# Mixers, channel weights and q tails fetched by GpSimd transfers that cast to fp16, in a fused attention and phase-mixing kernel

## Chip, cores and metric

One core of one Trainium2 chip. The metric is the device time of one execution in microseconds (us); lower is better.

## What is computed

Inputs are fp32. q, k and v have the shape batch 8, heads 8, sequence 576, head width 64. The matrices are theta and channel (512 x 512) and the two token mixers r and i (576 x 576). The reference, cut to what matters:

```python
kv = np.einsum('bhsd,bhse->bhde', k, v)          # linear attention
out = np.einsum('bhsd,bhde->bhse', q, kv)
rms = np.sqrt(np.mean(out * out, axis=-1, keepdims=True) + 1e-06)
x = out / rms * g_norm                           # then heads side by side: (8, 576, 512)

theta = x @ w_theta
zr, zi = x * np.cos(theta), x * np.sin(theta)
y = np.einsum('ts,bsd->btd', w_tok_r, zr) + np.einsum('ts,bsd->btd', w_tok_i, zi)
u = x + y
result = u + np.maximum(u @ w_ch, 0.0)
```

## The kernel before, in words

**Tiles.** A batch's 576 rows are four tiles of 128 and a tail of 64. Heads go in four pairs. For each pair kv is a product of fp32 k and v (L549). q is cast to fp16 into `qcast` (cast_q, L498, its tail L504, from the staging tile `ql`) and turned (`qT`): for batches 0 to 3 on TensorE (L645, tail L778), from batch 4 on by transposing DMAs (L519, L525). Then, by tile, come the product raw (L582), its square on ScalarE (sq), the sum on VectorE (ss), the power -1/2 on GpSimd (rt, L600 and L604; batch 0 uses a square root on ScalarE and a reciprocal instead), the scaled x (L616) and its transpose `xT` (L805, L814). Batches 0 and 1 do this by pairs of heads for the four full tiles (by_pair, with names like raw0h, sq1h, rt1h, xTps1h), and by tile for the tail alone. `phase` makes theta (`th`, L858, L863), rounds it with `pt` on ScalarE (L870) and `f` and `fa` on VectorE, takes two sines on ScalarE (`tr`, L893, tail L901) and multiplies (`z`, L911). `mix` sums `y` over the mixers (L954) and adds x (`uT`, L965). `channel` multiplies uT by `wch` (`vps`, L1012), turns uT back (`ups`, L1003, copied to `u`, L1019; for batches U_FROM = 4 to 6 by transposing DMAs, L1041, into `ub`), adds (`ot`, L1023) and stores (L1030, L1035).

**Weights.** `chunk` (L404) loads each weight in fp32 pieces on SP's queue into eight staging slots `wst`: four of theta, five for each mixer, four of the channel matrix. `cast` writes each piece to fp16 on ScalarE (L414), VectorE (L416) or GpSimd (L420): theta to `wth`; a mixer's first 512 columns to `wnat` (rows 512 to 575: `wnatl`) and its last 64 columns to `wtt`; the channel matrix to `wch`. `mixer_step` turns the mixers on TensorE (`wTps`, L477) and copies them to the nine tiles `wT` (L487).

**Order.** Nothing is ordered by hand. `Weave` (L59) is a planner that runs while the program is built: each step has costs on one or several engines, a due time from the table DUE, what it needs, and the buffers that it takes and frees. It picks step by step, with a model of engines and DMA, and `in_traced_order` then ties every engine to this order. At run time an engine that waits holds all that stands behind it in its order. SP issues all loads, stores and DMA transposes, at most eight in flight in the plan's model; loads keep the order of their due times. [...]the square root serves batch 0's norms, and the sine table is loaded once (`table`, L461) after all five square roots of batch 0, its tail's included. Products with no use (`warm`, L340) fill the gaps of TensorE up to a planned time, to keep its clock up.

**Loads before.** SP issues batch 0 (q, k, v of four pairs), then theta's four pieces with q, k, v of batch 1's first pair between them, batch 1's q tail, the five pieces of mixer r, batch 0's q tail, mixer i, the rest of batch 1, the first pair of batch 2 and its tails, the channel matrix, and so on.

Of the kernel before, what the change touches and what calls it, by code (L numbers as in the profile page):

```python
# [17 lines left out]

PERIOD = 26.33
START = 4.0  # L20
DUE = {
    "load": (-15.39, 8.44),
    "theta": (0.94, 0),
    "mixers": (12.3, 6.02),
    "wch": (33.66, 6.0),
    "wT": (20.94, 1.64),
    ("phase", 0): (19.67, 0.63),
    ("mix", 0): (28.29, 4.94),
    ("channel", 0): (31.53, 7.53),
    ("phase", 1): (11.06, 3.64),  # L30
    ("mix", 1): (31.8, 5.47),
    ("channel", 1): (54.0, 10.9),
    ("first", 1): (-21.76, 0.88),
    "first": (-9.27, 0),
    "cast": (27.66, 1.46),
    "turn_q": (-15.49, 0.49),
    "attention": (-2.25, 1.53),
    "norm": (0.56, 4.11),
    "turn": (5.47, 0.91),
    "phase": (18.31, 3.54),  # L40
    "mix": (52.55, 3.41),
    "channel": (67.54, 4.08),
}
# [3 lines left out]
    "rt": 6, "x": 9, "xT": 3, "pt": 2, "f": 2, "fa": 2, "tr": 2, "uT": 2, "u": 3, "ub": 1, "ot": 3,  # L47
    "wst": 8, "z0": 2, "z1": 2, "z2": 2, "z3": 2, "z4": 2,
}
BANK = {"th": "mm", "y": "mm", "vp": "mm", "pu": "tp", "px": "tp"}  # L50
QUAD = 2
Q_DMA = 4
U_FROM = 4
X_FROM = 8
MIX_AFTER = 3
WCH_AFTER = 8


class Weave:  # L59
# [7 lines left out]

    SLACK = {"PE": 0.141, "ACT": 0.031, "DVE": 0.084, "POOL": 0.1, "SP": 0.05}
    MARGIN = {"PE": 0.027, "ACT": 0, "DVE": 0.564, "POOL": 0.1, "SP": 0.0}
    LANES = 8  # L70
    BEGIN = {"PE": 1.6, "ACT": 3.2, "DVE": 1.7, "POOL": 2.5, "SP": 0.73}
    WARM = 72.3
    COLD = 5.0
    URGENT = 5.7
    AHEAD = 0.27
    HOLD = 3.61
    DRAIN = 0.095
# [21 lines left out]
    def run(self):  # L99
        done, free, last = {}, dict(self.BEGIN), {}  # L100
        dma_free, port_free, log = 0.0, 0.0, []
        landed = [0.0] * self.LANES
        hot, streak, form = False, self.BEGIN["PE"], 0
# [21 lines left out]
        while ready:  # L125
            best = {}
            for t in ready:
                (name, engines, due, fn, needs, makes, uses, dma) = t
                if any(not self.slots[tag] for (tag, _) in makes):
                    continue  # L130
                at = max([done[n] for n in needs], default=0.0)
                for (tag, _) in makes:
                    at = max(at, min(self.slots[tag]))
                if dma is not None:
                    at = max(at, landed[-self.LANES])
                for (e, cost, lat, port) in engines:
                    new = e == "PE" and self.ARRAY[port] != form
                    clear = free[e] + self.DRAIN if new else free[e]
                    start = max(clear, at + self.MARGIN[e], port_free if port is True else 0.0)
                    if name[0] == "warm" and start > self.WARM:  # L140
                        continue
                    if due < self.URGENT:
                        start = max(clear, start - self.AHEAD)
                    best.setdefault(e, []).append(
                        (start, due + self.HOLD * new, max(at, port_free) if port is True else at, t, cost, lat, port)
                    )
# [32 lines left out]
            if dma is not None:  # L179
                (first, took) = dma  # L180
                dma_free = max(start + first, dma_free) + took
                end = dma_free + 0.2
                landed.append(end)
            done[name] = start + cost if name[0] == "warm" else end
# [34 lines left out]
def kernel(  # L219
# [75 lines left out]
    for i in range(2):  # L295
        kl = const.tile([P, H, D], FP32, tag=f"kl{i}", name=f"kl{i}")
        vl = const.tile([P, H, D], FP32, tag=f"vl{i}", name=f"vl{i}")
        for t in (kl, vl):
            nc.gpsimd.memset(t[T:P], 0.0)
        tails.append((kl, vl))  # L300
    gcol = const.tile([P, 1], FP32, tag="gcol")
    root_d = const.tile([1, 1], FP32, tag="root_d")
    nc.vector.memset(root_d[:], math.sqrt(D))
    wth = wpool.tile([P, NK, C], FP16, tag="wth", name="wth")
    wch = wpool.tile([P, NK, C], FP16, tag="wch", name="wch")
    wnat = [wpool.tile([P, NF, SF], FP16, tag=f"wnat{i}", name=f"wnat{i}") for i in range(2)]
    wnatl = [wpool.tile([P, SF], FP16, tag=f"wnatl{i}", name=f"wnatl{i}") for i in range(2)]
    wtt = wpool.tile([P, NT, 2, T], FP16, tag="wtt", name="wtt")
# [22 lines left out]
    def dma(took):  # L331
        return (1.85, took)

# [13 lines left out]
    def load(b, hp):  # L347
        pair = slice(2 * hp, 2 * hp + 2)

        def part(kind, src):  # L350
            def fn(e):
                if kind == "q" or b >= QUAD:
                    t = sb(kind, [P, 2, NF, D], FP32, f"{kind}{b}_{hp}")
# [25 lines left out]
        for (i, (kind, src)) in enumerate((("q", q), ("k", k), ("v", v))):  # L379
            full = kind == "q" or b >= QUAD  # L380
            weave.add((kind, b, hp), [sp(0.47)], due("load", b, hp) + 0.01 * i, part(kind, src),
                      makes=[(kind, f"{kind}{b}_{hp}")], dma=dma((0.82 if full else 0.78) + (1.0 if (kind, b, hp) == ("v", 0, 0) else 0)), load=True)
        if hp == (0 if b else HP - 1):
            for (i, (kind, src)) in enumerate((("kl", k), ("vl", v), ("ql", q))):
                if b < QUAD and kind != "ql":
                    continue
                weave.add((kind, b), [sp(0.64)], due("load", b, hp) + (0.04 if b else 1.15) + 0.01 * i,
# [6 lines left out]
    def load_weights():  # L394
# [31 lines left out]
        at = due("load", 0, HP - 1) + 1.0  # L426
        mixers = due("load", MIX_AFTER // HP, MIX_AFTER % HP) + 1.0
        for kc in range(NK):
            chunk(("wst", kc), moe_w_theta[kc * P:(kc + 1) * P, :], at + 0.01 * kc)
            cast(("wth", kc), ("wst", kc), wth[:, kc, :],  # L430
                 lambda kc=kc: st["wst", kc][:, 0:C], due("theta", 0, kc), FOLD)
        use = due("mixers", 0, 0)
        for (i, w) in enumerate((moe_w_tok_r, moe_w_tok_i)):
            for j in range(NT):
                name = ("wmix", i, j)
                rows = P if j < NF else T
                chunk(name, w[0:SF, :].rearrange("(p j) s -> p j s", j=NF)[:, j, :] if j < NF
                      else w[SF:S, :], mixers + 0.1 + 0.1 * i + 0.01 * j)
                cast(("wnat", i, j), name, wnat[i][:, j, :] if j < NF else wnatl[i][0:T],
                     lambda name=name, rows=rows: st[name][0:rows, 0:SF], use + i)  # L440
                cast(("wtt", i, j), name, wtt[0:rows, j, i, :],
                     lambda name=name, rows=rows: st[name][0:rows, SF:S], use + i)
        for kc in range(NK):
            chunk(("wcs", kc), moe_w_ch[kc * P:(kc + 1) * P, :],
                  due("load", WCH_AFTER // HP, WCH_AFTER % HP) + 1.4 + 0.01 * kc)
            cast(("wch", kc), ("wcs", kc), wch[:, kc, :],
                 lambda kc=kc: st["wcs", kc][:, 0:C], due("wch", 0, kc))

# [16 lines left out]
    def mixer_step(n):  # L465
# [16 lines left out]
        def keep(e):  # L482
# [3 lines left out]
            else:  # L486
# [3 lines left out]
        weave.add(("wTps", n), [pe(0.282)], at, turn,  # L490
                  needs=[("wnat", n // NF, j) for j in range(NT)] if n < 2 * NF
                  else [("wtt", i, j) for i in range(2) for j in range(NT)], makes=[("tp", name)])
        weave.add(("wT", n), [act(S), dve(0.38, True)], at, keep, needs=[("wTps", n)], uses=[name])


    def cast_q(b, hp):
# [6 lines left out]
        def tail(e):  # L503
            nc.vector.tensor_copy(qcast[b % 2][:T, NF], st["ql", b][:])  # L504

        first = [("qc", f"qc{b}")] if hp == 0 else []
        more = [] if hp == 0 else [f"qc{b}"]
# [3 lines left out]
                  uses=[f"q{b}_{hp}"] + more)  # L511
        if hp == 0:
            weave.add(("qcl", b), [dve(0.33, True)], at + (0.1 if b else 9.0), tail,
                      needs=[("ql", b)], uses=[f"ql{b}", f"qc{b}"])
# [123 lines left out]
    def turn_q_pair(b, hp, at):  # L638
# [3 lines left out]
        def turn_q0(e):  # L642
            t = st[pq] = ps("tp", [P, SF], FP16, pq)
            for j in range(NF):
                nc.tensor.matmul(  # L645
                    t[:, j * P:(j + 1) * P], qcast[b % 2][:, j, pair, :], ident16[:],
                    is_transpose=True, start=(j == 0), stop=(j == NF - 1),
                )

        def keep_q0(e):  # L650
# [6 lines left out]
            else:  # L657
                nc.vector.tensor_copy(t, src)

        weave.add((pq,), [pe(0.226)], at, turn_q0, needs=[("qc", b, hp)], makes=[("tp", pq)],  # L660
                  uses=[f"qc{b}"])
        weave.add(("qT", b, hp), [act(SF), dve(0.35, True)], at, keep_q0, needs=[(pq,)],
# [324 lines left out]
    def channel(b, ti):  # L987
# [64 lines left out]
        elif ti == 0:  # L1052
            for kc in range(NK):
# [5 lines left out]
        weave.add((vp,), [pe(0.866) if full else pe(0.436, "H")], at + 0.01, product,  # L1059
                  needs=uTs + [("wch", kc) for kc in range(NK)] + ([] if pu_on else us),  # L1060
                  makes=[(BANK["vp"], vp)], uses=[f"uT{b}"])
# [68 lines left out]
```

## Time and profile before

| | |
|---|---|
| median of 18 runs | 218.98 us (217.85 to 221.1) |
| the profiled execution | 218.53 us, span 216.7 us |
| granted TensorE clock | 1.000 |
| DMA | 46.82 MB, mean 216 GB/s; SP's queue busy for 76.9% of 16 engines' span |
| loads of q, k, v: 256 KB each | 4.8 to 5.5 us from issue to landing |
| `ql` loads: 8 of 128 KB in pieces of 256 bytes | 5.0 us |
| GpSimd instructions in all | 93, of which 35 are powers of 1.75 us |

The table's DMA times are medians from issue to landing, and contain the queue: eight transfers share the 16 DMA engines. In the time lines of the profile a row has the start and the length in us, the engine (SPq is SP's queue), the line, the operation, the tile written and the tile read, and the shape. In the lists of groups a row ends with busy time, mean length in ns, and idle time in front of it with what ended it. TensorE's products are pipelined, so the sum of groups is more than the engine's own time.

### The profile page before, as it was taken

Reading aid. Unit: us, or ns where it says so; the run is one execution under the profiler, and the core shown is the slowest. Engines: PE = TensorE matmul, PEld = TensorE weight load, DVE = VectorE, ACT = ScalarE, POOL = GpSimd, SP = SyncE. Lnnn points to the kernel's source line nnn. Section 1 sums busy time; section 2 is a strip of 40 time slices with the busy share of each in tenths; the row PEclk is TensorE's granted clock in tenths of the full one; section 3 lists DMA queues with packets and bytes.
Section 4 is the critical chain, followed back from the end, with each engine's and each line's share of the span. In section 5 each row is a group of like instructions: output and inputs, shape, how many; then the busy total and the mean of one; then the engine's idle time right before and its main releaser. Section 6 shows DMA issues by size and latency. Waiting matters only on the chain.

```text
span 216.7 us, 5976 instructions
## 1 busy us (share of the span) xinstructions
PE 204.1 (94%) x2361; PEld 144.0 (66%) x2361; DVE 181.9 (84%) x368; ACT 154.9 (71%) x304; POOL 80.4 (37%) x93
## 2 busy tenths in 40 slices
PE   7688789999999999999999999999999999999992
PEld 5575347875767666876776776866675756677560
DVE  2296789899989899989998999999899899973652
ACT  2185989987993979889859997886886776930031
POOL 8001510762025630773257425655454763000000
PEclk9999999999999999999999999999999999999999
DMA  5999799999977988999896989992723232525524
GB/s 202 367 382 294 242 332 346 197 352 327 242 249 218 260 281 266 158 292 301 242 222 175 330 254 204 266 292 64 156 53 145 77 73 60 185 48 51 194 75 167
DMA packets 59007, 46.82 MB, mean 216 GB/s; under 512 B 29156, under 2 KB 50660, under 8 KB 58980
## 3 DMA queue, kind: packets, MB, share of 16 engines
q1 hardware_dynamic: 58976, 46.45, 76.9%
q8 instruction: 18, 0.29, 0.6%
q14 instruction: 9, 0.07, 0.1%
q10 hardware_dynamic: 4, 0.00, 0.0%
HBM read 33.06 MB, written 9.44 MB: 196 GB/s over the span
## 4 chain that ended last, share of the span: by engine, by line
PE 63%; ACT 12%; DVE 8%; DMA 8%; POOL 4%; issue 2%; SPq 0%; DVEq 0%; ACTq 0%
PE y L954 25%; PE vps L1012 13%; PE th L858 8%; PE kv L549 6%; DMA wst<-in_moe_w_theta_dram 3%; DMA k<-in_k_dram 3%; PE xTps L805 3%; PE raw L582 3%; ACT pt L870 2%; PE ups L1003 2%; DMA v<-in_v_dram 2%; ACT tr L893 2%; DVE ss L593 2%; POOL rt1h L717 2%; ACT tr L901 2%; DVE x L616 2%
## 5 line engine op out<-in xcount | busy, mean ns | idle before, releaser
L954 PE MATMUL y<-wT,z 128*128 128x320 f16 (+1 forms) x576 | 77.3, 286 | 0.4 <-DVE uT L965 0.4
L954 PEld LDWEIGHTS <-z 128*128 128x128 f16 x576 | 54.9, 98 | 16.4 <-issue 1.2
L604 POOL TENSOR_TENSOR rt<-ss,mhalf 128x8 f32<-128x8 f32 x31 | 54.3, 1752 | 2.6
L1012 PE MATMUL vps<-wch,uT 128*128 128x512 f16 (+1 forms) x192 | 36.5, 344 | 0.0
L965 DVE SCALAR_TENSOR_TENSOR uT<-y,gcol,xT 128x320 f16<-128x320 f32 (+1 forms) x48 | 29.2, 611 | 7.0 <-PE y L954 6.9
L600 POOL TENSOR_SCALAR ss<-ss 128x8 f32<-128x8 f32 x31 | 9.6, 309 | 68.5 <-DVE ss L593 67.7
L858 PE MATMUL th<-wth,xT 128*128 128x512 f16 x128 | 31.7, 379 | 0.7 <-DVE f L874 0.7
L870 ACT ACTIVATE pt<-th,magic_t 128x512 f32<-128x512 f32 (+1 forms) x40 | 25.7, 642 | 6.7 <-PE th L858 5.7
L1019 ACT COPY u<-ups 128x512 f16<-128x512 f16 (+1 forms) x28 | 14.4, 520 | 19.5 <-PE ups L1003 19.3
L874 DVE SCALAR_TENSOR_TENSOR f<-pt,th 128x512 f32<-128x512 f32 (+1 forms) x40 | 24.9, 626 | 2.9 <-ACT pt L870 2.5
L549 PE MATMUL kv<-v,k 128*64 128x64 f32 (+1 forms) x672 | 25.3, 222 | 2.2 <-DMA v<-in_v_dram 2.2
L549 PEld LDWEIGHTS kv<-v,k 128*64 128x64 f32 (+1 forms) x672 | 22.4, 136 | 6.7 <-issue 4.6
L814 ACT ACTIVATE xT<-xTps,gcol 128x512 f16<-128x512 f16 (+1 forms) x32 | 20.1, 630 | 7.9 <-PE xTps L805 7.8
L893 ACT ACTIVATE tr<-fa,pio_t 128x512 f16<-128x512 f32 x32 | 22.7, 718 | 1.8 <-DVE fa L881 1.7
L616 DVE TENSOR_TENSOR x<-raw,rt 128x512 f16<-128x512 f32 x32 | 21.8, 682 | 2.5 <-POOL rt L604 2.3
L593 DVE TENSOR_REDUCE ss<-sq 128x8 f32<-128x512 f32 x32 | 21.5, 677 | 2.4 <-ACT sq L589 2.1
L893 ACT ACTIVATE tr<-f 128x512 f16<-128x512 f32 x32 | 19.7, 630 | 3.2 <-DVE f L874 3.1
L1012 PEld LDWEIGHTS <-uT 128*128 128x128 f16 (+1 forms) x192 | 14.8, 102 | 10.3 <-issue 0.2
L911 DVE TENSOR_TENSOR z<-x,tr 128x1024 f16<-128x1024 f16 (+1 forms) x32 | 19.5, 616 | 0.8 <-ACT tr L893 0.4
L1023 DVE SCALAR_TENSOR_TENSOR ot<-vps,u 128x512 f32<-128x512 f32 (+1 forms) x28 | 17.0, 606 | 2.4 <-PE vps L1012 2.0
L858 PEld LDWEIGHTS <-xT 128*128 128x128 f16 x128 | 11.4, 98 | 11.4 <-ACT xT L814 1.2
L589 ACT ACTIVATE sq<-raw 128x512 f32<-128x512 f32 x32 | 18.8, 592 | 0.0
(103 smaller groups left out, 259.4 us busy)
## 6 DMA issues: line engine op xcount, KB each, us to landing
q<-in_q_dram SPq DMA_DIRECT2D x32, 256.0 KB, 5.5
out_dram<-ot SPq DMA_DIRECT2D x32, 256.0 KB, 2.5
k<-in_k_dram SPq DMA_DIRECT2D x24, 256.0 KB, 5.2
v<-in_v_dram SPq DMA_DIRECT2D x24, 256.0 KB, 4.8
k<-in_k_dram SPq DMA_DIRECT2D x8, 288.0 KB, 6.0
v<-in_v_dram SPq DMA_DIRECT2D x8, 288.0 KB, 6.1
wmix<-in_moe_w_tok_r_dram SPq DMA_DIRECT2D x4, 288.0 KB, 6.8
wmix<-in_moe_w_tok_i_dram SPq DMA_DIRECT2D x4, 288.0 KB, 3.7
```

Source lines behind the costliest of these rows:

```text
L549: nc.tensor.matmul(kvp[r * D:(r + 1) * D, hp, :], kt, vt, start=(j == 0), stop=(j == (NT if b >= QUAD else NS) - 1),)
L593: nc.vector.reduce_sum(out=t[:], in_=st[sq][:].rearrange("p (h e) -> p h e", h=H), axis=mybir.AxisListType.X,)
L604: nc.gpsimd.tensor_tensor(out=r[:], in0=t[:], in1=mhalf[:], op=ALU.pow)
L616: nc.vector.tensor_tensor(out=t[:].rearrange("p (h e) -> p h e", h=H), in0=st[raw][:].rearrange("p (h e) -> p h e", h=H), in1=st[rt][:].un ...
L814: nc.scalar.activation(out=st["xT", b][:, :, cols], in_=st[px][:, :, 0:cols.stop - cols.start], func=AFT.Copy, scale=gcol[:],)
L858: nc.tensor.matmul(t[:], xT[:, kc, :], wth[:, kc, :], start=(kc == 0), stop=(kc == NK - 1),)
L870: nc.scalar.activation(out=t[:], in_=st[th][:], func=AFT.Identity, bias=magic_t[:])
L874: nc.vector.scalar_tensor_tensor(out=t[:], in0=st[pt][:], scalar=MAGIC, in1=st[th][:], op0=ALU.subtract, op1=ALU.subtract,)
L893: nc.scalar.activation(out=t[:, which, :], in_=src[:], func=AFT.Sin, scale=-RAD, bias=0.0 if bias is None else bias[:],)
L954: nc.tensor.matmul(st[y][:, c, :], z[:, kc * P:(kc + 1) * P], wT[m][:, cols], start=(c == 0 and m == 0) if open_sums else m == 0, stop=m = ...
L965: nc.vector.scalar_tensor_tensor(out=st["uT", b][:, chunks, cols], in0=st[y][:], scalar=gcol[:], in1=st["xT", b][:, chunks, cols], op0=ALU ...
L1012: nc.tensor.matmul(t[half], uT(kc), wch[:, kc, r * n:(r + 1) * n], start=(kc == 0), stop=(kc == NK - 1),)
```

## The change

The mixers, the channel matrix and the q tails of batches 2 to 7 come by DMAs that GpSimd issues and that cast on the way, straight into the fp16 tiles. The staging pieces of the mixers and of the channel matrix are gone, and so are their casts; `wst` has four slots for theta alone. `wnat` now holds all 576 columns; the last 64 are copied on chip to `wtt`, in two steps for each mixer. A mixer is two transfers (128 partitions x 2304 elements, and 64 x 576), the channel matrix two, a q tail one: twelve in all. A `hold`, a copy of one column from a named v tile, stands in GpSimd's order ahead of the mixers (v of batch 0, pair 2) and of the channel matrix (v of batch 2, pair 0), so that they are issued only when that tile has landed. The q loads themselves stay on SP (Q_SOFT = 0).

The planner's DMA model gets a second queue (`Transfers`): GpSimd's transfers run at half pace, and SP's at half pace beside them. The planner's due times and its other constants are changed too, and with them the whole order: theta's four pieces and batch 0's q tail now come directly behind batch 0, then the rest of batch 1 and batch 2. Batch 3's output is now turned by DMA as well (U_FROM 3).

In the built program GpSimd's order is: hold, mixer r (two transfers), mixer i (two), two wtt copies of mixer i, two powers of batch 1, hold, the q tail of batch 2, the two channel transfers, the other powers of batch 1, and from there powers with the q tails of batches 3 to 7 between them. ScalarE has all four theta casts, and ahead of its first and second `pt` the two wtt copies of mixer r.

```diff
-U_FROM = 4
+U_FROM = 3
-MIX_AFTER = 3
+MIX_AFTER = 2
 WCH_AFTER = 8
+Q_SOFT = 0
+QL_SOFT = 1
...
-    "wst": 8, "z0": 2, "z1": 2, "z2": 2, "z3": 2, "z4": 2,
+    "qh": 6, "wst": 4, "z0": 2, "z1": 2, "z2": 2, "z3": 2, "z4": 2,
...
+    def soft(took):
+        return (2.4, took, True)
+
+    def hold(name, due, after):
+        def fn(e):
+            t = st[after]
+            nc.gpsimd.tensor_copy(late[:], t[:, 0, 0:1] if len(t.shape) == 3 else t[:, 0, 0, 0:1])
+        weave.add(name, [("POOL", 0.2, 0.22, False)], due, fn, needs=[after],
+                  uses=["{}{}_{}".format(*after)])
...
+                if kind == "ql" and QL_SOFT and b > 1:
+                    def fetch(e):
+                        nc.gpsimd.dma_start(
+                            out=qcast[b % 2][0:T, NF], in_=q[b, :, SF:S, :].rearrange("h s d -> s h d")
+                        )
+                    weave.add(("qcl", b), [("POOL", 0.56, 0.56, False)], due("load", b, 0), fetch,
+                              needs=[("qc", b, 0)], uses=[f"qc{b}"], dma=soft(0.9))
                     continue
...
-            for j in range(NT):
-                name = ("wmix", i, j)
-                rows = P if j < NF else T
-                chunk(name, w[0:SF, :].rearrange("(p j) s -> p j s", j=NF)[:, j, :] if j < NF
-                      else w[SF:S, :], mixers + 0.1 + 0.1 * i + 0.01 * j)
-                cast(("wnat", i, j), name, wnat[i][:, j, :] if j < NF else wnatl[i][0:T],
-                     lambda name=name, rows=rows: st[name][0:rows, 0:SF], use + i)
-                cast(("wtt", i, j), name, wtt[0:rows, j, i, :],
-                     lambda name=name, rows=rows: st[name][0:rows, SF:S], use + i)
...
+            def main(e, i=i, w=w):
+                nc.gpsimd.dma_start(
+                    out=wnat[i][:], in_=w[0:SF, :].rearrange("(p j) s -> p j s", j=NF)
+                )
+
+            def rest(e, i=i, w=w):
+                nc.gpsimd.dma_start(out=wnatl[i][0:T], in_=w[SF:S, :])
...
+            weave.add(("wnat", i), [("POOL", 0.56, 0.56, False)], use + 0.1 + i, main,
+                      needs=["hold_mix"], dma=soft(3.4))
+            weave.add(("wnatl", i), [("POOL", 0.56, 0.56, False)], use + 0.2 + i, rest,
+                      needs=["hold_mix"], dma=soft(0.5))
+            weave.add(("wtt", i, 0), [act(P * 2), dve(0.3, True), pool(P * 2)], use + 8, part(0),
+                      needs=[("wnat", i)])
+            weave.add(("wtt", i, 1), [act(T), dve(0.1, True), pool(T)], use + 8, part(1),
+                      needs=[("wnatl", i)])
...
+        for h in range(2):
+            def fetch(e, h=h):
+                nc.gpsimd.dma_start(
+                    out=wch[:, 2 * h:2 * h + 2, :],
+                    in_=moe_w_ch[h * SH:(h + 1) * SH, :].rearrange("(k p) c -> p k c", p=P),
+                )
```

## The prediction

> **What bounds the kernel now.** I read the page's busy shares first, then the busy time of each engine in stretches of 10 us, then the time lines of SP, ScalarE, GpSimd and VectorE over the first 45 us, then the chain that ended last. Shares first:
>
> ```profile
> PE 204.1 (94%) x2361; PEld 144.0 (66%) x2361; DVE 181.9 (84%) x368; ACT 154.9 (71%) x304; POOL 80.4 (37%) x93
> L340 PE MATMUL warm<-kvbd 128*128 128x256 f16 x42 | 10.1, 315 | 3.0 <-DVE root_d L303 1.5 <-ACT kvbd L678 0.7 <-DVE f L874 0.3
> ```
>
> TensorE is busy for 94%, and 10.1 us of that is the filler product (warm), which computes nothing. Where the rest is lost is told by the stretches (columns: PE, weight load, DVE, ACT, POOL busy, clock, DMA share, GB/s):
>
> ```profile
> 0.00:10.00 10.00, 6.75 (x96) 5.27 (x97) 2.52 (x13) 1.54 (x3) 4.89 (x15) 1.00 0.79 276
> 10.00:20.00 10.00, 8.65 (x164) 6.62 (x162) 8.41 (x20) 7.37 (x21) 0.62 (x1) 1.00 1.07 348
> 20.00:30.00 10.00, 8.14 (x73) 4.55 (x71) 7.12 (x15) 8.77 (x21) 4.07 (x8) 1.00 0.90 268
> 30.00:40.00 10.00, 9.03 (x166) 6.83 (x165) 8.71 (x22) 9.26 (x21) 0.92 (x3) 1.00 1.15 307
> 50.00:60.00 10.00, 10.00 (x139) 6.79 (x138) 9.69 (x21) 8.85 (x17) 0.12 (x1) 1.00 0.98 278
> 190.00:200.00 10.00, 10.00 (x81) 7.73 (x79) 5.41 (x10) 1.48 (x3) 0.00 (x0) 1.00 0.40 54
> ...
> ```
>
> The reader is to see two regimes. Up to 40 us TensorE has gaps, ScalarE is the fullest engine and the DMA engines are full. From 50 us on TensorE is at 9.6 to 10.0 in every stretch, so a cast saved on VectorE or ScalarE there moves nothing. The end is set by when the full regime begins and by how much TensorE work it holds. In the start-up, SP and ScalarE show why it begins late:
>
> ```profile
> 12.27 0.33 SPq L404 DMA_DIRECT2D wst<-in_moe_w_theta_dram x1
> 13.81 4.14 SPq L404 DMA_DIRECT2D wmix<-in_moe_w_tok_r_dram x5
> 21.07 0.62 SPq L373 DMA_DIRECT2D ql<-in_q_dram x1
> ```
>
> ```profile
> 23.63 1.14 ACT L414 ACTIVATE wnat<-wmix 128x512 f16<-128x512 f32 x2
> 30.12 1.28 ACT L461 ACT_TABLE_LOAD   x1
> 32.35 1.14 ACT L893 ACTIVATE tr<-f 128x512 f16<-128x512 f32 x2
> ```
>
> The q tail of batch 0 is issued only at 21.07, behind five mixer chunks that waited for staging slots. Through it the tail's norm is late (its product raw at 27.99), through that the switch to the sine table (30.12), and every sine waits for the table: the first at 32.35, the last about 43.0.
>
> **The part that removes work.** ScalarE loses six wnat casts (0.63 us each) and three wtt (0.25): 4.5 us between 21.6 and 29.7, then three wch (1.8 us). It gains two theta casts (it now has all four, 0.63 each) and two wtt copies (0.3 and 0.2 estimated from their 256 and 64 columns beside wtt's 0.25). VectorE loses 1.4 us of mixer casts, one theta cast (0.37) and six of eight q-tail casts (6 x 0.41 = 2.5 us); GpSimd loses 3.6 us of casts. On the path I count only what falls before the sines; q-tail casts lie under full TensorE and count nothing (if that cover were gone: 2.5 us). SP loses 20 issues.
>
> **The part that moves loads.** The first twelve loads are the same and end at 13.01. Loads land 0.75 us apart (11.52, 12.26, 13.01). Theta's last chunk landed at 19.32, with three loads of batch 1 between the chunks. Now the four chunks follow batch 0 directly: 16.0 if alone, 19.0 if the mixers take half of the DMA engines from about 13. Batch 0's q tail is next: 20 to 21 instead of 24.26. The mixers start when v of pair 2 has landed (about 10.8, between its neighbours' 9.99 and 11.52) plus a tiny GpSimd copy and the time from issue to first data, for which I take 2 us: 13. DMA moved 350 to 380 GB/s there; at half of that, the first mixer's 1.18 MB takes 6.5 us and lands at 19.6 to 20.5, the second at 27 to 28, before: 29.6. All of q, k, v of batch 1 come ahead of where they were (the total is 10.6 MB at 350 GB/s, about 31 us, against 36.6).
>
> **The new start-up, step by step.** In the built program's order the first theta product waits for the last x transpose. That stood behind a kv product of batch 1 that waited for its load (18.59); this kv now comes after the theta products. I take th at 20.3 instead of 20.94. ScalarE's first pt is ready at 21.3; the wtt copy now ahead of it waits for the first mixer (20.5), just hidden. Three th at 0.86 us, the tail's transpose, the fourth th: tail product raw at 24.0 instead of 27.99. From raw to the table took 2.1 us, and there is one more qT copy (0.5) ahead now: table at 26.7, first sine at 28.4 instead of 32.35. That is 4 us gained, but not all is kept: from the first to the last sine ScalarE took 10.6 us nearly without idle time, and the built order puts two wT copies, one xT, one sq and one qT copy more into that stretch (five at 0.5 to 0.58, 2.7 us). Last sine at about 41.7 instead of 43.0; ScalarE is the bound of the start-up, and what is late next is batch 1's last pair (square on ScalarE, sum on VectorE, 2.0 us of power on GpSimd, scale, transpose), by the same count 46 instead of 49.03.
>
> As a marker I take the first theta product of batch 1, at 50.35. Counting every product issued before it at the pace the trace shows (0.86 us for four of 512 columns, 1.22 for nine of 320, 1.05 for 36 small kv), 29.5 us of TensorE work lay before it and 28.9 lie before it now. By the chain above it comes at 47.7: 2.65 earlier, less 0.6 of work not yet done, 2.05. The other marker, the last step of the first two y sums (45.6, with 25.0 done), comes at 42.3 with 25.2 done: 3.4. I take the middle, **-2.8 us**.
>
> **TensorE work.** Batch 3's output transposes move from TensorE to DMA (U_FROM 4 to 3): four groups of four products, 0.22 each in the chain of waits, **-0.9 us**, on the full engine. Against it stand four VectorE adds that read the transposed tile (684 instead of 606 ns, 0.3 us, hidden) and four transposes on SP (2.5 us to land each), ahead of the next loads; batches 4 to 6 already do this without TensorE gaps, so I take nothing.
>
> **Waits added.** Twelve transfers now stand in GpSimd's queue. Behind each q tail is a pair of power instructions (0.31 + 1.75 us) for which VectorE's x waits. All x waits for rt total 2.3 us in the whole run, and GpSimd is busy for 37%. The trace of before has no GpSimd transfer; the bound from above is 1 us for each of six issues, 6 us, from below 0. The nearest row is SP's own issue of a q tail, 0.62 us, and a TensorE that has other products ready, so I take 0. The hold before wch stands in front of the last two powers of batch 1 until v of batch 2 lands (41.41 before, about 36 now); the powers are due near 39 to 41, so it is hidden; if that load came no sooner, it would cost some 2 us.
>
> One rule speaks against this change. VectorE and GpSimd already stop each other in this trace:
>
> ```profile
> 26.39 0.79 DVE L504 CAST qcast<-ql 64x512 f16<-64x512 f32 x1
> ```
>
> ```profile
> 26.29 0.62 POOL L420 TENSOR_SCALAR wnat<-wmix 128x512 f16<-128x512 f32 x1 [0.31 <-DMA wmix<-in_moe_w_tok_i_dram]
> ```
>
> This cast takes 0.41 us elsewhere; here it waited for the GpSimd cast beside it, 0.38 us. The Trainium skill, "SBUF — State Buffer", the box on the "DVE blocks DMA" trap, says more: descriptors of GpSimd's transfers are written through the port that VectorE's two-port modes lock, and a transfer of some 620 ns alone became 3100 ns beside a copy. By the row a transfer starts at most 0.4 us late and the first mixer lands at 20.9: no loss. By the rule it starts 2.5 us late, at 15.5, lands at 23, and the pt queue behind the wtt copy slips 1.7 us: the sum would be 217.0. No run here shows the rule; I go by the row, since VectorE's instructions are short[...], and keep 217.0 in the range.
>
> **Sum.** The profiled execution took 218.53, of which 216.7 is the span. -2.8 - 0.9 = -3.7: span 213.0, execution 214.8. The median of the runs is 218.98, 0.45 above the profiled one: **215.3**.
>
> **Rivals.** (1) *The casting transfer is slow* (slower than before). If the DMA engines pass cast data at half the pace, the first mixer needs 13 us and lands at 26.5. ScalarE's wtt copy then holds all four pt, th is out of slots, the table and every sine follow: 5.2 us after 21.3, 220.5. It decides from a landing of 21.3 + 3.7 = 25.0. For it: nothing in the trace shows a cast in flight, the DMA engines are already full at that time, and the SP loads queue beside it. Against: the bytes read are the same and the bytes written are halved. (2) *The gain is hidden*: batch 1's chain (its loads, casts and powers) ends no sooner, ScalarE's extra copies eat the earlier table, and only the transposes remain: -0.9, with up to 0.8 more, 217.3 to 218.1, call it 217.8. For it: DMA share of about 1.0 up to 60 us. (3) *More is kept*: theta is unshared (16.0), all casts go early and the whole 4 to 5 us of the table survive: -5 - 0.9, 213.0. For it: full TensorE afterwards keeps every us.
>
> **How the numbers follow.** Forecast 0.55 (its own range 214 to 217), rival 1 0.18, rival 2 0.15, rival 3 0.12. A measurement of this kernel tells apart about 0.3%, 0.66 us. Faster takes the forecast, rival 3, and most of rival 2: 0.76; same 0.07; slower 0.17. The range reaches over rivals 2 and 3 and the near part of rival 1: 212.2 to 219.6.
>
> **What would show it.** Right: the table load near 27 instead of 30.12; th of batch 0 at about 20; the first theta product of batch 1 near 47.7; TensorE full from there; ups groups x96. Wrong: a first ScalarE wtt copy that waits for a mixer past 25 (rival 1); the table early and batch 1's theta still at 50 (rival 2); x waiting for rt by much more than 2.3 us in all (the port rule, or GpSimd's issue cost). A gap of TensorE over 2 us after 60 us would break the ground of the sum, that the later part is full.

## The result and the profile after

The changed kernel took **216.31 us** (median of 8 runs, 215.82 to 216.97); the kernel before, run beside it, 218.86 us (48 runs). The ratio is 0.988, with a 95% interval of 0.986 to 0.991: 2.55 us are gained, where 3.7 were forecast. The profiled execution took 216.68 us, span 214.9 (before 218.53 and 216.7). All ratios leave out the few executions that lie more than 1.5% above the fastest of the same kernel.

First the shares, from the page of the changed kernel:

```profile
PE 205.4 (96%) x2358; PEld 145.5 (68%) x2358; DVE 178.1 (83%) x357; ACT 149.9 (70%) x291; POOL 86.4 (40%) x101
```

VectorE and ScalarE are less busy (181.9 to 178.1 and 154.9 to 149.9). GpSimd lost casts too, but with twelve transfers to issue it is busier (80.4 to 86.4). That alone says nothing about the end. The stretches do (same columns as before):

```profile
20.00:30.00 10.00, 9.62 (x121) 6.43 (x120) 7.68 (x18) 7.91 (x16) 0.63 (x2) 1.00 1.03 295
30.00:40.00 10.00, 9.51 (x175) 7.65 (x175) 8.66 (x20) 9.85 (x23) 5.39 (x6) 1.00 1.12 323
50.00:60.00 10.00, 10.00 (x127) 6.67 (x124) 9.34 (x19) 9.37 (x18) 0.40 (x1) 1.00 0.63 153
...
```

TensorE has fewer gaps between 20 and 40 us (8.14 and 9.03 before), and not through more filler: without `warm` it is busy for 15.1 us of these 20, before for 12.7. ScalarE is at 9.85 in 30 to 40: it is still the bound of the start-up. ScalarE's time line shows the start-up itself:

```profile
15.37 0.63 ACT L489 ACTIVATE wth<-wst 128x512 f16<-128x512 f32 x1 [0.97 <-DMA wst<-in_moe_w_theta_dram]
...
20.83 0.40 ACT L524 COPY wtt<-wnat 128x256 f16<-128x256 f16 x1 [1.48 <-DMA wnat<-in_moe_w_tok_r_dram]
21.80 0.69 ACT L983 ACTIVATE pt<-th,magic_t 128x512 f32<-128x512 f32 x1 [0.57 <-PE th L971]
...
26.75 1.28 ACT L562 ACT_TABLE_LOAD   x1
...
28.59 0.62 ACT L1006 ACTIVATE tr<-f 128x512 f16<-128x512 f32 x1
...
40.71 1.03 ACT L1014 ACTIVATE tr<-fa,pio_t 64x256 f16<-64x256 f32 x2
41.64 0.61 ACT L586 COPY wT<-wTps 128x576 f16<-128x576 f16 x1
...
42.86 0.59 ACT L805 ACTIVATE sq1h<-raw1h 128x512 f32<-128x512 f32 x1
```

The table comes at 26.75 instead of 30.12 and the first sine at 28.59 instead of 32.35. The wtt copy waits for the first mixer, but the pt behind it then waits for its own product. The last sine of batch 0 ends at 41.74; before it ended at 43.01:

```profile
41.99 1.02 ACT L901 ACTIVATE tr<-fa,pio_t 64x256 f16<-64x256 f32 x2
```

GpSimd issues the mixers here:

```profile
11.07 0.18 POOL L384 COPY late<-v 128x1 f32<-128x1 f32 x1 [5.40 <-DMA v<-in_v_dram]
11.59 0.79 POOL L510 DMA_DIRECT2D wnat<-in_moe_w_tok_r_dram  x1 [0.34 <-issue]
```

An issue takes 0.56 to 0.79 us; VectorE is at 83% over the whole span. The first mixer landed at 20.81, the second at 25.07. The DMA queues of 11.6 to 25.6 us (packets, MB, share of the 16 engines; q0 is GpSimd's, q1 is SP's):

```profile
q1 hardware_dynamic: 2565, 2.73, 58.2%
q0 software_dynamic: 448, 1.33, 47.7%
```

The profile counts a cast transfer in the fp16 bytes that it writes: q0's 1.33 MB are the 2.65 MB of the two mixers in fp32. So 5.38 MB were read in 14.0 us, 384 GB/s. The same view for 11.6 to 15.0 us has no q0 at all (q1 has 104.9%), and for 15.0 to 20.8 us it has

```profile
q0 software_dynamic: 267, 0.87, 74.9%
q1 hardware_dynamic: 604, 0.62, 34.3%
```

The mixers' data thus began to move 3.4 us after the first issue, and then had most of the DMA engines. SP's queue shows why they were left to it:

```profile
13.12 1.10 SPq L420 DMA_DIRECT2D v<-in_v_dram  x1
21.12 0.64 SPq L433 DMA_DIRECT2D ql<-in_q_dram  x1
```

SP issues nothing from 14.2 to 21.1 us. Its next load is batch 1's q tail, there is one `ql` buffer, and batch 0's tail stays in it until its cast at 20.68. What a second buffer would do was not tried.

Two markers are used below. The first theta product of batch 1 starts at 48.76 (before 50.35). From it to the last product TensorE takes 161.55 us (before 210.31 and 212.19 as the last product's start: 161.84). So most of the gain of this pair of profiles (1.59 of 1.88 us) came before 50 us.

### The profile page after: what moved, and what is told of

Its sections match the earlier page's. It is cut to its first block, busy times and chain, and to the rows that moved or that the text cites. A ratio compares the mean times of both kernels' runs of the same rounds, so it can differ in the third digit from the quotient of the medians.

```text
span 214.9 us, 5949 instructions
## 1 busy us (share of the span) xinstructions
PE 205.4 (96%) x2358; PEld 145.5 (68%) x2358; DVE 178.1 (83%) x357; ACT 149.9 (70%) x291; POOL 86.4 (40%) x101
## 4 chain that ended last, share of the span: by engine, by line
PE 55%; DVE 22%; DMA 9%; ACT 5%; POOL 5%; issue 3%; SPq 1%; DVEq 0%; ACTq 0%
PE y L1067 22%; PE vps L1125 10%; PE th L971 8%; PE kv L655 5%; DVE f L987 4%; DMA wst<-in_moe_w_theta_dram 3%; DVE ot L1136 3%; DMA vl<-in_v_dram 3%; DVE uT L1078 3%; POOL rt L710 3%; DMA k<-in_k_dram 3%; PE raw L688 2%; PE xTps L918 2%; DVE z L1024 2%; DVE x L722 2%
## 5 line engine op out<-in xcount | busy, mean ns | idle before, releaser
L655 PE MATMUL kv<-v,k 128*64 128x64 f32 (+1 forms) x672 | 26.0, 227 | 0.4 <-DMA v<-in_v_dram 0.4
L655 PEld LDWEIGHTS kv<-v,k 128*64 128x64 f32 (+1 forms) x672 | 23.3, 141 | 3.7 <-issue 2.6
L1132 ACT COPY u<-ups 128x512 f16<-128x512 f16 (+1 forms) x24 | 12.1, 513 | 17.5 <-PE ups L1116 17.4
L1024 DVE TENSOR_TENSOR z<-x,tr 128x1024 f16<-128x1024 f16 (+1 forms) x32 | 19.6, 617 | 1.6 <-ACT tr L1014 1.4
L599 DVE CAST qcast<-q 128x512 f16<-128x512 f32 x32 | 13.4, 419 | 5.7 <-DMA q<-in_q_dram 5.7
```

Source lines behind the costliest of these rows:

```text
L655: nc.tensor.matmul(kvp[r * D:(r + 1) * D, hp, :], kt, vt, start=(j == 0), stop=(j == (NT if b >= QUAD else NS) - 1),)
L1024: nc.vector.tensor_tensor(out=t[:], in0=xb.unsqueeze(1).broadcast_to((P, w, C)), in1=st[tr][:, 0:w, :], op=ALU.mult,)
```

## Experiments

In most of these the order of the changed kernel was written out as a list and then edited by hand, so that the planner could not move anything else. Differences in us are differences of the ratio to the kernel before, times 218.9. The control is e1. Single executions of one program differ in the start-up (the first theta product of batch 1 comes at 48.76 in the changed kernel and at 48.12 in e1, the same program), so small effects are read from the timed runs, and profiles are used for the place.

**e1, the control.** No edit: the changed kernel's order as a list.

> The changed kernel once more, its order written out as a list, as the reference on this chip for the runs beside it. All theories: 216.3 (216.0 to 216.8), 2.5 below the kernel before.

Measured 215.99 us, ratio 0.9888 (0.9848 to 0.9928); first theta product of batch 1 at 48.12, then 161.57 us. The list is as good as the planner. Five of its six runs lie between 215.82 and 216.05; the sixth, 218.42, widens the interval to 0.9 us on either side.

**e2, batch 3 turned back on TensorE again.**

```diff
-U_FROM = 3
+U_FROM = 4
...
-('ud', 3, 0..3) on SP
+('ups3_n',) on PE, ('u3_n',) on ACT, ahead of each ('vps3_n',)
```

> The changed kernel with every engine's order kept, but batch 3's output turned on TensorE again (16 products of 128 columns and 4 ScalarE copies come back, 4 DMA transposes go). Theory (TensorE is full there, so its work counts one to one): 0.9 more than the changed kernel, 217.2 (216.9 to 217.5). Rival (the start-up made the whole gain, and there is slack later): 216.3.

Measured 217.14 us, ratio 0.9926 (0.9897 to 0.9955), 0.83 us above the control; its lowest run, 216.98, lies above five of the control's six. In this order the transposes are worth what they take on TensorE.

**e3, ScalarE's casts put back.** Six casts of 512 columns go from a theta piece into an unused tile: two ahead of the first pt, two ahead of the second, one ahead of the tail's square and one ahead of its root.

```diff
+nc.scalar.activation(out=spare[:], in_=st["wst", 0][:, 0:C], func=AFT.Copy)   # six times
```

> The changed kernel with its order kept, and six ScalarE casts of 512 columns (0.63 each) into a spare tile put back where the mixer casts stood: two ahead of the first pt, two ahead of the second, one ahead of the tail's square, one ahead of its root. Nothing of the result changes. Theory (the casting transfers gain by emptying ScalarE ahead of the sine table): the table comes 2 to 2.5 late (some of the six lie in idle time), and all of it reaches the end: 218.3 (217.6 to 218.8). Rival (the gain is the q tail's place in the loads; the casts were hidden): table within 0.8 of 26.75, time 216.3 to 216.9.

Measured 217.92 us, ratio 0.9958 (0.9934 to 0.9983): 1.5 us above the control. ScalarE's time line in this run:

```profile
20.29 1.29 ACT L663 ACTIVATE spare<-wst 128x512 f16<-128x512 f32 x2
...
27.77 1.28 ACT L827 ACT_TABLE_LOAD   x1
```

The table is 1.7 us later than in the control (26.07), the first theta product of batch 1 1.5 us later (49.64), and the rest takes 161.3 us, about as in the control. 3.8 us of casts on ScalarE at this place are worth 1.5 us: the largest single part that was found.

**e4, all wT copies on VectorE.** Four of the nine copies of turned mixers stand on ScalarE among the sines, and the ninth released the last step of the first two y sums.

```diff
-('wT', 4|5|7|8) on ACT
+('wT', 4|5|7|8) on DVE
```

> The changed kernel with its order kept, but all nine wT copies on VectorE, as in the kernel before (the changed kernel has four of nine on ScalarE, 0.63 each, between the first sine and the last y of batch 0). Theory (these copies ate the earlier sine table: the last y step waited for the ninth copy at 44.2): last y step of the first two sums 1 to 1.7 earlier, time 215.3 (214.8 to 215.9). Rival (batch 1's chain over GpSimd's powers and the loads holds the start-up): within 0.3 of 216.3.

Measured 216.46 us, ratio 0.9892 (0.9868 to 0.9916): nothing. The wait of y that the trace shows for this copy is not the one that sets the time.

**e8, the kv copy of the fourth pair ahead of theta's cast.** In the profile above ScalarE waits 0.97 us for theta's first piece, and this small copy stands behind it.

```diff
-('wth', 0), ('bd', 0, 3), ('rt0', 2) on ACT
+('bd', 0, 3), ('rt0', 2), ('wth', 0) on ACT
```

> The changed kernel with its order kept but for one place: on ScalarE the copies of kv of batch 0's last pair and the root of its third pair go ahead of the first theta cast, which waited for theta until 15.34. Theory (theta, sharing the DMA engines with the mixer from 13 on, held this copy and with it the last pair's x): the last x transpose of batch 0 and the first th come 0.8 to 1.2 earlier than 19.85 and 20.90, but pt then waits for the mixer's wtt copy (20.8), so only part passes on: 215.9 (215.4 to 216.3). Rival (theta's own last cast sets th): th within 0.3 of 20.9, 216.3.

Measured 217.24 us, ratio 0.9906 (0.9876 to 0.9937): no gain either. In its profile the copy no longer waits for theta, but 0.66 us for its own kv product, and th comes at 21.03.

**e12, the wtt copies of mixer r on GpSimd.**

```diff
-('wtt', 0, 0), ('wtt', 0, 1) on ACT, ahead of ('pt0_0',) and ('pt0_1',)
+the same on POOL, ahead of ('wtt', 1, 0)
```

> Order of the changed kernel kept; the two wtt copies of mixer r go from ScalarE, where they stand ahead of pt and waited 1.5 us for the mixer in the profile, to GpSimd beside those of mixer i. Theory (that wait sits on ScalarE's path to the table): table 0.6 us earlier (the copies took 0.4 and 0.2), time 215.5. Rival: the wait and the copies lie beside the wait for the first theta product, nothing changes: 216.0.

Measured 216.48 us, ratio 0.9871 (0.9828 to 0.9915), 0.4 us below the control and within the intervals. In its profile ScalarE's wait for the mixer is a wait of 2.45 us for the first theta product instead, pt at 22.08. The wait for the mixer was covered.

**e11, theta cast in flight as well.** The factor that ScalarE's cast put on theta is left out in this kernel, so only its time says something.

```diff
-chunk(("wst", kc), ...); cast(("wth", kc), ..., FOLD)
+hold("hold_th", at, ("v", 0, 1))
+nc.gpsimd.dma_start(out=wth[:, 2*h:2*h+2, :], in_=moe_w_theta[...])   # two halves
```

> Order of the changed kernel kept, but theta too comes by two casting transfers of GpSimd, issued when v of batch 0, pair 1, has landed, straight into wth: ScalarE loses its four theta casts (2.5 us before the table), SP four issues; the wtt copies of mixer r go to GpSimd as in the next run. Theory (ScalarE's occupancy before the table sets the start-up, as the run with six casts put back says: 1.5 us for 3.8 us of casts): 2.5 us off ScalarE gains about 1 us, 215.0. Rival: theta and the mixers now share the DMA engines with batch 0's loads, theta lands later than 17.5 and the mixers later than 25, and the time is 216 to 219.

Measured 216.40 us, ratio 0.9854 (0.9816 to 0.9891), 0.4 us below e12 on the same chip, not told apart. Theta landed at 19.02 (16.45 in e12), the mixers at 21.78 and 24.94. ScalarE was rid of 2.5 us of casts and waited 2.97 us for th instead. ScalarE's time is worth something behind the first theta product (e3); ahead of it no worth was seen (e11 and e12), within about 0.9 us.

**e10, mixers issued later.**

```diff
-MIX_AFTER = 2
+MIX_AFTER = 4
```

> Order of the changed kernel kept; GpSimd's hold ahead of the mixers waits for v of batch 1, pair 0, instead of v of batch 0, pair 2, so that the mixers are issued at about 20 us instead of 11 to 13. The first should then land at 26 to 28 us instead of about 20.5. Theory (the prediction's first rival, which decides at a landing of 25.0): ScalarE's copy into wtt holds all pt behind it, the table and every sine follow by about 6 us, and the time becomes 220 to 222. Rival: batch 1's first loads come sooner and their work fills the gap, so that no more than 2 us are lost: 216 to 218.

Measured 222.92 us, ratio 1.016 (1.012 to 1.020): 5.9 us above the control. ScalarE in this run:

```profile
25.15 0.40 ACT L781 COPY wtt<-wnat 128x256 f16<-128x256 f16 x1 [7.00 <-DMA wnat<-in_moe_w_tok_r_dram]
25.46 0.68 ACT L1240 ACTIVATE pt<-th,magic_t 128x512 f32<-128x512 f32 x1
```

TensorE, and the stretch from 20 to 30 us (columns as above; the third from the end is the clock):

```profile
26.92 1.87 PE L1228 MATMUL th<-wth,xT 128*128 128x512 f16 x4 [4.51 <-DVE f L1244]
20.00:30.00 10.00, 5.49 (x34) 2.66 (x33) 2.38 (x5) 3.72 (x8) 2.05 (x5) 0.76 0.94 197
```

The wait of 7.00 us holds all pt behind it (theta's first product was there at 19.54 to 20.4), the table comes at 31.44, and batch 1's first theta at 54.41. The first rival's mechanism exists, and the landing of the mixer is what keeps it away. A second loss comes with it: TensorE stands still for 4.51 us, and the granted clock then falls, to 0.76 in this stretch and 0.89 in the next (four th products take 1.87 us instead of 1.03). So the rival decides earlier than the 25.0 of the prediction, which counted the slip alone: with a landing of 25.13 the kernel is 3.4 us slower than before. A straight line between 20.81 (2.55 faster) and 25.13 would put the point at an estimated 22.7; it is rough, since pt still had 0.57 us to spare at 20.81.

**e6, the q tail moved in the kernel before.** Batch 0's q tail is due behind theta and ahead of the mixers; nothing is cast in flight, and the planner orders anew.

```diff
-(0.04 if b else 1.15)
+(0.04 if b else 1.025)
```

> The kernel before, planned anew with one due time changed: batch 0's q tail is loaded ahead of the mixers, directly behind theta, all staging and casts kept. Theory (the tail's place opens the way to the sine table, but ScalarE is still full of casts and batch 1 still comes behind the mixers): table 1.5 to 2.5 earlier than 30.12, time 0.3 to 0.9 less than before, 218.2. Rival (the order is the whole start-up gain): 1.6 less than before, 217.3. Second rival (mixers then come later, and y waits for them): no gain or a loss, 218.9 or more.

Measured 224.52 us, ratio 1.023 (1.019 to 1.027). The table came at 26.04, 4 us earlier than before, and the kernel lost 5 us. SP's queue, the stretch from 30 to 40 us, and TensorE show where:

```profile
13.20 9.47 SPq L373 DMA_DIRECT2D ql<-in_q_dram  x2
22.71 2.64 SPq L404 DMA_DIRECT2D wmix<-in_moe_w_tok_r_dram  x5
```

```profile
30.00:40.00 10.00, 7.82 (x77) 5.90 (x75) 6.03 (x14) 9.19 (x20) 2.30 (x5) 0.51 1.07 349
```

```profile
31.27 0.30 PE L477 MATMUL wTps<-ident,wnatl 128*128 128x128 f16 x1 [0.74 <-ACT wnatl L414]
...
36.95 2.19 PE L549 MATMUL kv<-v,k 64*64 64x64 f32 x36 [0.27 <-DMA v<-in_v_dram]
```

The new order puts batch 1's q tail directly behind batch 0's, and both need the one `ql` buffer. SP waits until the first is cast (21.60 to 22.0), and the mixers, which it issued at 13.81 before, go out at 22.71. They are then cast between the sines, and their turning waits for the casts (1.5 us). TensorE's granted clock is 0.51 in this stretch: 36 small kv products take 2.19 us, elsewhere 1.26. All five executions had a mean clock of 0.964 to 0.974, the kernel before 0.98 or more. Batch 1's first theta is at 54.83, 4.5 us later than before, and 1.8 us more are lost behind it. An early table alone is not the gain: what comes through the same queue and the same ScalarE after it must be early too. What the place of the q tail is worth by itself this run does not tell, since SP's wait, the late casts and the clock came together; what brought the clock down here was not tried.

**e5, U_FROM = 3 alone in the kernel before.** The planner orders anew.

```diff
-U_FROM = 4
+U_FROM = 3
```

> The kernel before with one change, U_FROM 3: batch 3's output turned by DMA. The instruction order is the same up to the middle of the kernel. Theory: 0.9 less than the kernel before, 218.0 (217.6 to 218.3). Rival (the DMA transposes hold up loads or stores on SP): 218.5 to 219.5.

Measured 220.54 us, ratio 1.007 (1.004 to 1.009): 1.45 us lost, not 0.9 gained. The later part took 163.85 us. The chain that ended last (start, length, what):

```profile
142.63 0.81 PE vps L1012 x4
143.44 3.89 DMA k<-in_k_dram
...
147.33 0.41 DVE qcast L504
```

And SP's queue ahead of that load:

```profile
133.38 4.28 SPq L1041 DMA_TRANSPOSE ub<-uT  x3
...
143.44 0.41 SPq L354 DMA_DIRECT2D k<-in_k_dram  x1
```

Three transposes hold SP for 4.28 us, and k, v and q of the next batches are issued from 141 us on instead of from 134. TensorE then has 7.47 of 10 us in 150 to 160. The same edit is worth +0.8 us in one order and -1.45 in another; in e5 the chain runs through a load that SP issued late. In the changed kernel three of them hold SP even longer (5.30 us from 130.18), but q, k and v follow them directly, at 135.53; in e5 the k and v tails, a transpose and the q tail come between. The changed kernel has 20 fewer issues on SP, but that this is what makes the room was not tried by itself.

**e7 and e9, the q tails on SP and VectorE again.** e7 puts all six back, e9 those of batches 3 to 7.

```diff
-('qcl', b) on POOL
+('ql', b) on SP behind ('vl', b); ('qcl', b) on DVE behind ('qc', b, 1)
```

> The changed kernel with its order kept, but the q tails of batches 2 to 7 loaded by SP in fp32 and cast on VectorE again (6 casts of 0.41, six SP loads of 0.64 more, six GpSimd transfers less). Theory (they lie under a full TensorE): within 0.4 of 216.3. Rival A (VectorE's relief counts in the full part): 218.0 or more. Rival B (GpSimd's transfers cost, by their place ahead of the powers and by the port shared with VectorE): 215.5 or less.

> Order of the changed kernel kept; only the q tails of batches 3 to 7 go back to SP's queue and a cast on VectorE (2.0 us of casts and five 0.6 us issues on SP); that of batch 2 stays with GpSimd. Putting all six back had cost about 1.2 us more than the changed kernel in the fixed order. Theory A: that price was paid in the start-up, where batch 2's tail is queued on SP ahead of batch 2's loads; then this run is 216.0 to 216.3, and from the first theta product of batch 1 to the last product it takes 161.6 us. Theory B: it was paid later, under the full TensorE, through VectorE's casts and SP's queue; then this run is 217.0 to 217.3, and that stretch takes 162.5 us or more.

Measured 218.28 us, ratio 0.9936 (0.9908 to 0.9964), and 218.21 us, 0.9927 (0.9896 to 0.9958): 1.05 and 0.85 us above the control. Against e12, measured beside e9 on the same chip, e9 is 1.2 us longer. Theory B held. Both profiled executions (221.84 and 221.02 us) lay above their other runs because of events before 45 us: in e9 batch 0's q tail came late (the last section), in e7 TensorE stood still for 2.44 us at 37.9 without a cause that the profile shows, and in both the granted clock then fell (0.83 in 20 to 30 and in 40 to 50). From 50 us on it is 1.00 in both, and only the part behind the start-up is read. There the two traces agree step by step. From the end of the start-up (a product raw at 44.5 in e1) to the same product of batch 7 at 177.3, e9 loses 1.21 us against e1 and e7 1.36, in the same steps of 0.07 to 0.33 us at products that wait for VectorE. The two largest (0.32 near 63, 0.33 near 147 us) were followed: at the first the turn of batch 3's tail waits 0.40 us for the cast itself; the second is shown here, VectorE in e1:

```profile
141.47 0.42 DVE L856 CAST qcast<-q 128x512 f16<-128x512 f32 x1
141.80 0.42 DVE L1251 TENSOR_SCALAR fa<-f 128x512 int32<-128x512 int32 x1
142.13 1.28 DVE L1393 SCALAR_TENSOR_TENSOR ot<-vps,ub 128x512 f32<-128x512 f32 x2
```

and in e9:

```profile
145.89 0.42 DVE L857 CAST qcast<-q 128x512 f16<-128x512 f32 x1
146.22 0.41 DVE L863 CAST qcast<-ql 64x512 f16<-64x512 f32 x1
146.56 0.41 DVE L1252 TENSOR_SCALAR fa<-f 128x512 int32<-128x512 int32 x1
146.89 1.27 DVE L1394 SCALAR_TENSOR_TENSOR ot<-vps,ub 128x512 f32<-128x512 f32 x2
```

```profile
147.62 0.59 PE L1383 MATMUL vps<-wch,uT 128*128 128x512 f16 x2 [0.17 <-DVE ot L1394]
```

Without the cast, ot starts 0.66 us behind the cast of q; with it, 1.00. ot is what frees the accumulator that the next vps writes, and TensorE stands for the difference: the distance between the two vps there grows by 0.33 us.

## Why the prediction came out as it did

216.31 lies in the range of 212.2 to 219.6 and in the forecast's own 214 to 217, 1.0 us above the number. The direction and its cause were right: an earlier table, emptied ScalarE, fuller TensorE from 20 to 40 us. Two sizes were off, the start-up (1.8 us too much) and the q tails (1.0 us too little), and they partly cancel: that the number came within 1.0 us is in part luck.

- **th at 20.3**: 20.74, hardly earlier than the 20.94 before. The kv product of batch 1 was indeed out of the way, but ScalarE waited for theta's first piece with the fourth pair's kv copy behind it, so the fourth raw product of batch 0 came at 16.36 instead of 15.18. Taking theta's cast out of its way (e8) gained nothing.
- **Why the tail was late before**: the prediction put it to the mixer chunks that waited for staging slots. These account for SP's time up to 17.95; then SP waited 3.1 us more for the one `ql` buffer, which batch 1's tail held until its cast at 20.63. The same buffer stops SP in the changed kernel and in e6.
- **Mixers at 19.6 to 20.9 and 27 to 28**: 20.81 and 25.07, the first by luck. Its data was to start at 13.0 with half of the DMA engines; it started at 15.0 with 74.9%, while SP issued nothing. By the prediction's estimate from the rule of the Trainium skill, "SBUF — State Buffer", the "DVE blocks DMA" box, the start was to be at 15.5, which is near, and the landing at 23, which is not. Whether VectorE delayed the start, as the rule has it, or the DMA engines, which SP's loads filled until then, is not separated. Where the DMA engines had room, a busy VectorE alone did not show: in e10 a q tail issued at 77.61, with VectorE busy for all of the next 1.47 us, began to move at 79.08, and the mixer issued at 19.49, with VectorE mostly idle, after 1.50 us.
- **Table 26.7, first sine 28.4, last sine 41.7**: 26.75, 28.59, 41.74.
- **Start-up, -2.8**: this term was mis-sized. The step that failed is the one from ScalarE's last sine to batch 1. The last sine came as forecast (41.74), 1.3 us earlier than before; the prediction let the two chains behind it gain more than that, 2.65 and 3.3 us. The last pair's xT was to come at 46 and came at 47.1, the first theta of batch 1 at 48.76, not 47.7. Less the 0.6 us of work not yet done, that is 1.0 us instead of 2.05. The other marker, the last step of the first two y sums, came at 44.8, not 42.3: 0.8 earlier instead of 3.3, with 0.2 more work done, so about 1.0 too. The last pair's square is one place where time went: its product raw started at 41.23, and ScalarE came to the square at 42.86, behind the sine, a wT copy and an x transpose. That the copies alone are not the cause e4 shows; the rest is open. The lower of the two forecast markers would have been nearer than their middle, and still twice what came.
- **q-tail casts hidden, 0** (2.5 us if the cover were gone): wrong. e7 and e9 price them at about 1 us, some 0.24 for each cast of 0.41 (1.21 over five). "Busy for 10.00 of 10" does not mean that no wait counts: VectorE was at 9.96 in 120 to 130 too, and a step inserted ahead of ot holds TensorE. This is gain that the sum did not have.
- **TensorE work, -0.9**: 0.83 in e2. That the four transposes on SP cost nothing holds in this order alone; in the order of e5 they cost more than they save.
- **Waits added, 0**: x waits for rt 2.2 us in all (before 2.3). One power did start late: that of batch 1's third pair, at 41.99, some 0.8 us after its sum, behind the q tail and the two channel transfers that GpSimd issued from 39.68 on. The fourth pair, which ends the chain, did not wait for them, so no cost of the hold or of the issues is seen at the end.
- **Rivals.** The slow cast: refuted here by the read rate (384 GB/s) and the landing at 20.81, and shown to be real as a mechanism by e10, from an earlier point. The gain hidden: refuted, though closer than thought for the start-up alone. More kept: refuted; theta's last piece landed at 17.52, between the 16.0 and 19.0 of the prediction.

The parts do not sum exactly. 1.0 (start-up), 1.0 (q tails) and 0.8 (transposes) make 2.8 against 2.55 of the medians and 1.85 of the two profiled executions. In the profiles the part behind 50 us should be shorter by 1.0 + 0.8 - 0.6 = 1.2 us and is shorter by 0.3. Single executions differ by several tenths; whether the new order also gave something back there, by the four transposes or otherwise, is open. So is what the new order of the loads is worth without the casts, which e6 could not tell; e3 alone, with 1.5 us, comes to as much as the start-up gained.

## What to carry to other kernels

An engine that reads as full in every stretch can still be held by a second one that is nearly full: look at what frees its accumulators before a saved cast is put at nothing. When an early event is gained, follow the engine that must do the work behind it; if that engine is at 9.9 of 10, most of the gain is spent there. A queue that many steps share (here SP's) gives the same edit a different sign in a different order. Before an early load is put into such a queue, ask whether its buffer is free: one `ql` buffer stopped SP for 3 to 8 us in three orders.

## What was not expected of the hardware

Transfers that cast from fp32 to fp16 ran at the read rate of plain loads (384 GB/s above, beside 350 to 380 before). Where they share the DMA engines, the loads of the other queue become late and uncertain. Batch 1's first q, issued at 11.73 in the changed kernel, landed 12.5 us later, where the median of these loads is 5.2; in e12, issued at 11.79, it took 8.4. And batch 0's q tail, issued on SP at 10.1 to 11.1, was cast at 19.5 to 21.0 without any wait in seven profiled executions, and in three others VectorE waited for it, in the worst case

```profile
23.98 0.42 DVE L863 CAST qcast<-ql 64x512 f16<-64x512 f32 x1 [4.09 <-DMA ql<-in_q_dram]
```

That is the e9 execution, whose table then came at 29.57. Before, its load was issued at 21.07 and landed at 24.26, so the tail was late by its place; now it is late sometimes. What chooses was not tried.

TensorE's granted clock fell to half in four of the profiled executions, for about 3 to 10 us at a time. In e10, e9 and e7 TensorE had stood still for about 2 us or more shortly before (4.51, 1.93 and 2.44 us in one wait); in e6 its single waits were below 1 us. In the profiles of the kernel before and of the changed kernel the clock is 1.00 in every stretch up to 210 us. In e9 and e10 the late load thus cost more than the wait itself.
